# An attention and gated-MLP kernel with its whole instruction order given as a table instead of being planned at build time

## The chip, the cores and the metric

The kernel runs on one core of one Trainium2 chip. The metric is the device time of one execution in microseconds (us); lower is better. Three runs of the kernel before gave 678.15, 683.24 and 683.33 us, median 683.24 us.

## What is computed

One transformer layer on 2048 tokens of width 512, attention (32 heads of 16) and a gated MLP (hidden width 1792) side by side on the same normalised input, both added to the input:

```python
qkv = (x @ wqkv).reshape(B, S, 3, H, Dh).transpose(2, 0, 3, 1, 4)
scores = jnp.einsum("bhqd,bhkd->bhqk", q, k) * (Dh ** -0.5)
o = jnp.einsum("bhqk,bhkd->bhqd", softmax(scores), v)
attn = o.transpose(0, 2, 1, 3).reshape(B, S, D) @ wo
...
gate = x @ W_gate;  gate = gate * (gate > 0)
mlp = (gate * (x @ W_up)) @ W_down
...
xn = layernorm(x);  return x + attn(xn) + mlp(xn)
```

## The kernel before

**Tiling.** Queries are cut into 4 stretches of 512 columns (`c4`), heads into 4 groups of 8 (`gg`), each group into even and odd heads (`ee`), keys into 16 tiles of 128 (`kt`). That makes 32 blocks `(c4, gg, ee)` of 16 key tiles. For one key tile of one block, four heads are done side by side: four scores of 128 keys x 512 queries.

**Two ways to the exponential.** Most key tiles go through ScalarE (ACT): a *unit* is two of the four scores, put in one of two pairs of PSUM banks (`P_sc`, unit `u` uses pair `u % 2`), and one `activation(Exp)` of 128 x 1024 turns it into bfloat16 in a ring (L1546). There are 704 units. The other key tiles, 160 of 512, go through VectorE (DVE) and GpSimd (POOL): four evictions shift and clip a score into 16-bit integers whose bits are those of a bfloat16 (L1502, 640 of them), and two further additions (L1516 on POOL, a few on DVE at L1519) make shifted copies; all three patterns are multiplied with v, so that their sum approximates the exponential.

**TensorE (PE).** Every matmul of the stretch in the middle is on a quarter-wide tile, 64 rows x 32 columns, and loads its weights by separate instructions: four matmuls and four weight loads make one operation of the graph (L141 is the helper that records each of these matmuls; weight loads are at L1482 for scores, L1454 for the products with v, L934 for projections, MLP and output). An operation uses the upper or the lower 64 rows, and two operations on different halves can run together. A weight load is left out where the half still holds the same weights.

**Background work.** Between the units run projections of q and k, the MLP (`glu`), and output rows (`out_rows`), handed out in slots along the units. After each pair of blocks there is a chain of small steps, `normalise`: evict the sums to `o_sb` (L1364), DMA the row sums out (`rsum`, L1382 and L1388), merge even and odd heads by DMA (L1396), take reciprocals (L1403), DMA these into `rb` (L1405), spread them over partitions on DVE (L1417) and multiply (L1420). A q projection ends with an eviction and eight DMAs of 16 rows into `qT` (L982). All of these DMAs are issued from one queue, SyncE's (SP).

**What sets the order.** The kernel first records a graph: operations with an engine, a duration in ns, tiles read and written, a priority. `Graph.run` (L216) then plays a list scheduler over it at build time. It walks a model clock, takes on each engine the ready operation with the best key, picks buffer slots for tiles as it goes, and appends to one queue per engine. Its model has, for instance, 216 ns for an operation of PE, 917 ns for an exponential and a wire model for DMAs. `Graph.emit` works out which semaphore waits are needed for that order and writes the five instruction streams. Each engine executes its stream in order. `run` may also put single blank matmuls ("fill", L1564) into early gaps of PE; there are 7 in the program.

The score operation of unit `u` must wait until ACT has read unit `u - 2`, since both use one pair of banks. So on PE, every unit's scores carry a semaphore wait on ACT, and the work behind them in PE's stream waits too.

Of the kernel before, what the change touches and what calls it, by code (L numbers as in the profile page):

```python
# [49 lines left out]
EARLY = ()  # L50
# [4 lines left out]
TOGETHER = 0  # L55
# [32 lines left out]
QUADS = [0, 2, 5, 5, 6, 6, 4, 5, 6, 5, 5, 5, 6, 5, 5, 8, 5, 5, 4, 6, 6, 4, 6, 5, 5, 5, 5, 5, 5, 6, 5, 5]  # L88

# [43 lines left out]
class Op:  # L133
    __slots__ = ("eng", "dur", "fn", "deps", "order", "prio", "acq", "name", "idx", "start", "end",
                 "done", "left", "users", "signal", "sem", "val", "waits", "stream", "lat", "seq", "cseq", "hb", "after", "mode", "half", "bank", "urgent", "slack", "port",
                 "load", "wsrc", "wkey", "wwaits", "pair", "held")
# [9 lines left out]
class Graph:  # L146
# [5 lines left out]
    SWITCH = 107.0  # L152
    TO_POOL = 110.0
    ISSUE = 16.0
    FILL = 425.0
    NEAR = 20
    OWN = 90.0
    DMA_SLACK = 1000
    FILL_MIN = 230.0
    AHEAD_LOADS = 4  # L160
    EARLY = True
    REUSE = 5
    WIRE_LAT, WIRE_KB = 1300.0, 6.1
    WARM_AT, COLD = 7300.0, 2.0

    def __init__(self):
        self.ops = []
        self.fillers, self.nfill, self.twins = [], 0, []
        self.units = {}
# [46 lines left out]
    def run(self):  # L216
        ops = self.ops
        for o in ops:
            o.users = []
            o.held = []  # L220
        for t in {t for o in ops for t in o.acq} | {c for o in ops for t in o.acq for c in t.pool.cur if c is not None}:
            us = set(t.w + t.r)
            t.left = len(us)
            for o in us:
                o.held.append(t)
        for o in ops:
            if o.after is not None and int(o.after) > 0:
                o.order.add(self.units[min(int(o.after), len(self.units)) - 1])
            pre = set(o.deps) | o.order
            o.left = len(pre)  # L230
            for d in pre:
                d.users.append(o)
        cand = {e: [] for e in self.ENGS}
        free = {e: 0.0 for e in self.ENGS}
        self.queue = {e: [] for e in self.ENGS}
        for o in ops:
            if o.left == 0:
                cand[o.eng].append(o)
        n = 0

        def slot_for(t):

            best, second = None, None
            for i in (t.allowed if t.allowed is not None else range(len(t.pool.cur))):
                c = t.pool.cur[i]
                if c is None:
                    at = 0.0
                else:
                    at = release.get(c)
                    if at is None:  # L250
                        if c.left:
                            continue
                        at = release[c] = max(u.end for u in c.w + c.r)
                if best is None or at < best[0]:
                    best, second = (at, i), best
                elif second is None or at < second[0]:
                    second = (at, i)
            if t.pool.shared:
                held = any(c is not None and c.open > 0 for c in t.pool.cur)
                if t.extra:  # L260
                    if t.extra.slot is None:
                        return None
                elif t.open:
                    if held and not (self.EARLY and second is not None):
                        return None
                elif len(t.allowed) > 3 and (not held or any(b.slot is None and b.extra.slot is not None for b in self.twins)):
                    return second
            return best


        pe = {"mode": "full", "at": -1e9, "free": [0.0, 0.0]}
        last = {}

        known, release = {}, {}

# [8 lines left out]
        def ready(o):  # L284
            at = known.get(o)
            if at is None:
                at = known[o] = bound(o)
# [1314 lines left out]
```

## Time and profile before

| | |
|---|---|
| median of 3 runs | 683.24 us (678.15 to 683.33) |
| time of the profiled execution | 683.3 us |
| its span, first to last instruction | 681.3 us |
| granted TensorE clock | 1.000 |
| PE busy | 669.6 us (98%), 22355 matmuls |
| PE weight loads | 410.7 us (60%), 20975 |
| ACT busy | 659.9 us (97%), 721 instructions |
| DVE busy | 591.3 us (87%), 1001 |
| POOL busy | 334.6 us (49%), 345 |
| DMA, mean of the span | 42 GB/s |

Busy time is the union of the intervals in which an engine has an instruction under way, as the profiler records them. For matmuls the ends are modelled, so a busy PE is not a PE that streams at its peak. "Idle before" is the time between the end of an engine's last instruction and the start of the next, put down to what released it; "issue" means that the engine waited for nothing that the profile shows. A line of the timeline merges neighbours of one kind: start, length, engine, line, operation, tiles, and after the `x` how many.

### The profile page before, as it was taken

Reading aid. Unit: us, or ns where it says so; the run is one execution under the profiler, and the core shown is the slowest. Engines: PE = TensorE matmul, PEld = TensorE weight load, DVE = VectorE, ACT = ScalarE, POOL = GpSimd, SP = SyncE. Lnnn points to the kernel's source line nnn. Section 1 sums busy time; section 2 is a strip of 40 time slices with the busy share of each in tenths; the row PEclk is TensorE's granted clock in tenths of the full one; section 3 lists DMA queues with packets and bytes.
Section 4 is the critical chain, followed back from the end, with each engine's and each line's share of the span. In section 5 each row is a group of like instructions: output and inputs, shape, how many; then the busy total and the mean of one; then the engine's idle time right before and its main releaser. Section 6 shows DMA issues by size and latency. Waiting matters only on the chain.

```text
span 681.3 us, 46196 instructions
## 1 busy us (share of the span) xinstructions
PE 669.6 (98%) x22355; PEld 410.7 (60%) x20975; DVE 591.3 (87%) x1001; ACT 659.9 (97%) x721; POOL 334.6 (49%) x345
## 2 busy tenths in 40 slices
PE   8999999999999999989999999999999999999997
PEld 3456576565575765656665665556565666666664
DVE  8948999998998887989999788899989877889886
ACT  7999999999999999999999999999999999999995
POOL 3301445554455554645555564655456644435640
PEclk9999999999999999999999999999999999999999
DMA  7511011132201021110101011011200122120001
GB/s 217 79 37 28 19 39 39 40 95 67 86 12 28 24 63 36 26 47 12 45 4 36 27 49 49 24 25 28 52 6 17 32 59 60 42 52 21 23 13 34
DMA packets 51479, 28.78 MB, mean 42 GB/s; under 512 B 18840, under 2 KB 50328, under 8 KB 51288
## 3 DMA queue, kind: packets, MB, share of 16 engines
q1 hardware_dynamic: 51144, 25.70, 14.7%
q8 instruction: 169, 2.77, 1.8%
q14 instruction: 22, 0.18, 0.1%
q10 hardware_dynamic: 144, 0.13, 0.1%
HBM read 18.22 MB, written 2.10 MB: 30 GB/s over the span
## 4 chain that ended last, share of the span: by engine, by line
PE 94%; DVE 4%; DMA 1%; issue 1%; POOL 0%; DVEq 0%; SPq 0%
PE ps L141 94%; DVE qd L1502 1%; DVE stats L831 1%; DMA rb<-rrec 1%; DMA x_sb<-in_A_x_dram 0%; DVE xn_sb L854 0%; DVE mv L833 0%; DVE up_sb L1151 0%; DVE xnT L899 0%; PE ps L1275 0%; DVE qT L1086 0%; DVE xn_sb L1319 0%; DVE hT L1155 0%; DVE kT L992 0%; DVEq L605 0%
## 5 line engine op out<-in xcount | busy, mean ns | idle before, releaser
L1546 ACT ACTIVATE ring<-ps 128x1024 bf16<-128x1024 f32 x704 | 651.9, 1063 | 9.6 <-PE ps L141 8.4
L141 PE MATMUL ps<-qT,kT 64*32 64x512 bf16 x8192 | 473.6, 375 | 3.6 <-DVE qd L1502 1.8
L1516 POOL INT64_ADD qd<-qd x312 | 321.8, 1042 | 305.7 <-DVE qd L1502 189.2
L1502 DVE TENSOR_SCALAR qd<-ps 128x512 int16<-128x512 f32 x640 | 418.8, 684 | 52.1 <-PE ps L141 46.9
L141 PE MATMUL ps<-qd,v_aug 64*32 64x512 bf16 x3840 | 306.7, 375 | 0.5 <-issue 0.2
L141 PE MATMUL ps<-ring,v_aug 64*32 64x512 bf16 x2816 | 245.3, 375 | 0.8 <-issue 0.7
L1482 PEld LDWEIGHTS <-kT 64*32 64x32 bf16 x8164 | 182.2, 92 | 105.7 <-issue 26.1
L1454 PEld LDWEIGHTS <-v_aug 64*32 64x32 bf16 x5304 | 132.6, 92 | 58.9 <-issue 7.4
L141 PE MATMUL ps<-xnT,wus 64*32 64x512 bf16 x1792 | 136.4, 375 | 0.0
L141 PE MATMUL ps<-xnT,wgs 64*32 64x512 bf16 x1792 | 136.0, 375 | 0.1
L141 PE MATMUL ps<-Wd,hT 64*32 64x512 bf16 x768 | 59.5, 375 | 0.2 <-issue 0.2
L934 PEld LDWEIGHTS <-hT 64*32 64x32 bf16 x1792 | 45.8, 92 | 22.2 <-issue 3.9
L934 PEld LDWEIGHTS <-wgs 64*32 64x32 bf16 x1792 | 44.4, 92 | 22.3 <-issue 4.4
L934 PEld LDWEIGHTS <-wus 64*32 64x32 bf16 x1792 | 45.1, 92 | 19.5 <-issue 3.0
L141 PE MATMUL ps<-Wk,hT 64*32 64x512 bf16 x512 | 43.0, 375 | 0.0
L1151 DVE COPY up_sb<-ps 128x512 f32<-128x512 f32 x56 | 38.3, 684 | 5.3 <-PE ps L141 5.1
L1155 DVE SCALAR_TENSOR_TENSOR hT<-ps,up_sb 128x512 bf16<-128x512 f32 x56 | 38.2, 682 | 3.6 <-PE ps L141 3.4
L141 PE MATMUL ps<-Wv,hT 64*32 64x512 bf16 x512 | 40.3, 376 | 0.2 <-issue 0.2
L141 PE MATMUL ps<-xnT,Wq 64*32 64x512 bf16 x480 | 39.3, 375 | 0.0
L141 PE MATMUL ps<-Wo_p,x_sb 64*32 64x512 bf16 x480 | 37.8, 376 | 0.0
L141 PE MATMUL ps<-xnT,Wk 64*32 64x512 bf16 x480 | 35.7, 375 | 0.3 <-DVE xnT L899 0.3
L141 PE MATMUL ps<-Wv,xnT 64*32 64x512 bf16 x512 | 33.0, 375 | 0.4 <-issue 0.2
(83 smaller groups left out, 221.9 us busy)
## 6 DMA issues: line engine op xcount, KB each, us to landing
wus<-in_B_W_up_dram SPq DMA_DIRECT2D x38, 128.0 KB, 2.6
wgs<-in_B_W_gate_dram SPq DMA_DIRECT2D x38, 128.0 KB, 3.0
xr_sb<-in_A_x_dram SPq DMA_DIRECT2D x16, 128.0 KB, 2.3
qT<-qf SPq DMA_DIRECT2D x120, 16.0 KB, 2.5
o_sb<-o_sb SPq DMA_DIRECT2D x60, 32.0 KB, 2.5
out_dram<-xn_sb SPq DMA_DIRECT2D x15, 128.0 KB, 1.8
x_sb<-in_A_x_dram SPq DMA_DIRECT2D x8, 128.0 KB, 2.8
Wd<-in_B_W_down_dram SPq DMA_DIRECT2D x6, 128.0 KB, 2.3
```

What stands on the lines that cost most here:

```text
L141: return e.add_instruction(mybir.InstMatmult(name=e.bass.get_next_instruction_name(), engine=mybir.EngineType.PE, ins=[e.lower_ap(x), e.lo ...
L831: G.op("DVE", 580, lambda e, m=m: e.bn_stats(stats[:, m, :], xs(m)), reads=[t_xm[m]], writes=[t_st], prio=pr, order=last_xn if m == 4 and ...
L934: e.ldweights(w()[rows, 32 * j:32 * j + 32], tile_position=(rows.start, 32 * j))
L1151: G.op("DVE", 603, lambda e: e.tensor_copy(up_sb[:, tup.slot, :], bank_of(tu)), reads=[tu], writes=[tup], prio=-590)
L1155: G.op("DVE", 603, lambda e: e.scalar_tensor_tensor(out=hT[:, th.slot, :], in0=bank_of(tg), scalar=0.0, in1=up_sb[:, tup.slot, :], op0=ALU ...
L1454: e.ldweights(vs(j), tile_position=(64 * half, 32 * j))
L1482: e.ldweights(ks(m), tile_position=(64 * half, 32 * m))
L1502: G.op("DVE", 601, lambda e, j=j, tx=tx: e.tensor_scalar(qd[:, tq.slot, 512 * j:512 * j + 512], ps[:, BANK[tx.slot], :], IBIAS[3], 0.0, op ...
L1516: G.op("POOL", POOL_NS, lambda e, x=x, n=n: e.int64_add(x().bitcast(I64), raw().bitcast(I64), SHIFTS[n + 1] * LANES), reads=[ti, tq, t_lib ...
L1546: exp_ops[u] = G.op("ACT", ACT_NS, lambda e, tr=tr, k0=k0: e.activation(ring[:, tr.slot, :, :], ps[:, 4 * k0:4 * k0 + 2, :], ACTF.Exp, sca ...
```

## The change

The graph is recorded as before, operation for operation. `Graph.run`, its model constants and its tie-breaking rules are gone. In their place stands `Graph.follow`, which takes two tables: `ORDER`, the numbers of all operations in the order in which they are to be appended to the queues (`-1` is a blank matmul), and `SLOTS`, one character for each tile that needs a buffer, the number of the slot. It appends, and adds the dependences that follow from reusing slots and banks. `emit` is the same but for an unused line. The tables were worked out off line, with the fetch of TensorE's program in blocks counted in; how is not in the kernel.

```diff
-TOGETHER = 0
...
+ORDER = [
+    0, 3, 19, 1, 9, 51, 2, 4, 5, 10, 20, 7, 6, 14, 8, 17, 21, 22, 23, 24, 52, 25, 11, 53, 56, 26, 27, 54, 57, 60, 55, 28, 64, 58, 61, 68, 29, 59, 62, 65,
...
+SLOTS = [int(c, 36) for c in (
...
-    def run(self):
...
+    def follow(self, order, slots):
         self.queue = {e: [] for e in self.ENGS}
+        last, port, slots = {}, None, iter(slots)
+        for i in order:
+            if i < 0:
+                o = Op()
+                o.eng, o.fn, o.name, o.half, o.bank, o.urgent, o.stream, o.port = "PE", self.filler, "fill", None, None, 0, None, False
+                o.deps, o.order, o.acq = {}, set(), []
+                o.load, o.wsrc, o.wkey, o.wwaits, o.pair = None, (), None, (), None
+                self.ops.append(o)
+            else:
+                o = self.ops[i]
+            e = o.eng
             for t in o.acq:
                 if t.slot is not None:
                     continue
+                t.slot = next(slots)
+                c = t.pool.cur[t.slot]
                 if c is not None:
                     for u in c.w + c.r:
+                        if u.eng != e or e not in ("PE", "ACT"):
                             o.deps[u] = True
+                t.pool.cur[t.slot] = t
+            if e == "PE" and o.half is not None:
+                was = last.get(o.bank)
+                if was is not None and was.half != o.half:
+                    o.deps[was] = True
+                last[o.bank] = o
+            if o.port:
+                if e == "POOL" and port is not None:
+                    o.deps[port] = True
+                if e == "DVE":
+                    port = o
             o.seq = len(self.queue[e])
             self.queue[e].append(o)
...
-        G.fillers = [(P_b, 0, "pvz", blank_early, "full")]
-        G.run()
+        G.filler = blank_early
+        G.follow(ORDER, SLOTS)
         G.emit(nc, es)
```

Compared stream by stream, the two programs have the same instructions: 22354 recorded matmuls on both sides, 20860 separate weight loads before and 20888 after (reuse falls differently), 7 blank matmuls on both, 104 separate semaphore instructions on PE before and 128 after, the same 718 activations in the same order on ACT, the same operations on DVE, POOL and SP. The order differs on PE, DVE, SP and, slightly, POOL, from the first microseconds on. On SP, the eight `qT` DMAs of a projection, which mostly stood together before, are now mixed with weight loads and with the DMAs of `normalise`.

273 lines of the change are left out of this document (28 added, 245 removed), and 314 rows, old and new, of the table ORDER.

## The prediction

> **What bounds the kernel now.** I read the page's first part, then ACT's timeline over the whole span, then the waits.
>
> ```profile
> PE 669.6 (98%) x22355; PEld 410.7 (60%) x20975; DVE 591.3 (87%) x1001; ACT 659.9 (97%) x721; POOL 334.6 (49%) x345
> ```
>
> ```profile
> 620.00:640.00 20.00, 20.00 (x724) 12.78 (x672) 17.81 (x29) 20.00 (x23) 11.37 (x11) 1.00 0.05 13
> ```
>
> PE looks full (98%), but that is a busy time with modelled ends. In the windows of 20 us, the densest full one got 724 matmuls through (the first x). At that pace all 22355 would take 22355 / 724 x 20 = 618 us. The exponentials take longer, as these lines of ACT's timeline show (start, length, line, count, idle before):
>
> ```profile
> 10.32 1.96 ACT L1546 ACTIVATE ring<-ps 128x1024 bf16<-128x1024 f32 x2
> 12.44 1.02 ACT L1546 ACTIVATE ring<-ps 128x1024 bf16<-128x1024 f32 x1 [0.17 <-PE ps L141]
> 13.92 4.73 ACT L1546 ACTIVATE ring<-ps 128x1024 bf16<-128x1024 f32 x5 [0.46 <-PE ps L141]
> 19.21 12.95 ACT L1546 ACTIVATE ring<-ps 128x1024 bf16<-128x1024 f32 x14 [0.55 <-PE ps L141]
> 32.32 3.77 ACT L1546 ACTIVATE ring<-ps 128x1024 bf16<-128x1024 f32 x4 [0.17 <-PE ps L141]
> ...
> 131.57 36.33 ACT L1546 ACTIVATE ring<-ps 128x1024 bf16<-128x1024 f32 x39 [0.22 <-PE ps L141]
> 169.17 56.54 ACT L1546 ACTIVATE ring<-ps 128x1024 bf16<-128x1024 f32 x61 [1.27 <-PE ps L141]
> ...
> 264.17 11.46 ACT L1546 ACTIVATE ring<-ps 128x1024 bf16<-128x1024 f32 x12 [0.54 <-PE ps L141]
> ...
> 294.11 122.16 ACT L1546 ACTIVATE ring<-ps 128x1024 bf16<-128x1024 f32 x132 [1.61 <-PE ps L141]
> ...
> 604.16 67.61 ACT L1546 ACTIVATE ring<-ps 128x1024 bf16<-128x1024 f32 x73 [0.15 <-PE ps L141]
> 672.24 0.66 ACT L1291 ACTIVATE up_sb<-ps 128x256 f32<-128x256 f32 x2 [0.47 <-PE ps L141]
> ```
>
> ```profile
> 348.64 11.11 ACT L1546 ACTIVATE ring<-ps 128x1024 bf16<-128x1024 f32 x12
> ```
>
> ```profile
> 358.59 3.00 ACT L1546 ACTIVATE ring<-ps 128x1024 bf16<-128x1024 f32 x3
> ```
>
> ```profile
> ACT ring L1546 <- PE ps L141: 8.4, 20, 1.6
> PEld L1482 <- issue: 26.1, 84, 2.1
> PEld L934 <- issue: 18.8, 60, 1.0
> PEld L1454 <- issue: 7.4, 31, 0.5
> ```
>
> The span falls into a head of 10.3 us (before the first exponential), a stretch of 704 exponentials from 10.32 to 604.16 + 67.61 = 671.77, that is 661.45 us, and a tail of 681.3 - 671.8 = 9.5 us. The last two small timelines give ACT's own pace. The twelfth exponential of the run that begins at 348.64 begins at 358.59, so 11 steps take 9.95 us, 0.905 each; one alone takes 1.02 (row at 12.44), since neighbours overlap. Were ACT always fed, the stretch would take 1.02 + 703 x 0.905 = 637.2 us. So 24.2 us of it are lateness, and PE, which feeds ACT, is what ACT waits for. The kernel is bound by ACT (637 of 661), and the 24 us are PE arriving late although its sum (618) would fit. That is a question of order, which is what the change touches.
>
> Lateness has two parts. Twenty stops are visible: 8.4 us idle, and each also loses the overlap, 1.02 - 0.905 = 0.115 us, so 8.4 + 20 x 0.115 = 10.7 us. The other 13.5 us lie inside the runs: the run of 132 takes (122.16 - 1.02) / 131 = 0.925 a step, not 0.905.
>
> **What lies behind the stops.** Weight loads (PEld) are idle with nothing to wait for ("issue") 84 + 60 + 31 = 175 times, 52.3 us. Two of these, and then the stream between them and the program's own DMA queue:
>
> ```profile
> 168.76 0.09 PEld L934 LDWEIGHTS <-wgs 64*32 64x32 bf16 x4 [0.67 <-issue]
> ```
>
> ```profile
> 263.33 0.37 PE L141 MATMUL ps<-ring,v_aug 64*32 64x512 bf16 x1 [0.47 <-issue]
> 263.33 0.09 PEld L934 LDWEIGHTS <-hT 64*32 64x32 bf16 x4 [0.97 <-issue]
> ```
>
> ```profile
> 263.33:416.25 152.92, 150.37 (x5134) 94.12 (x4824) 136.31 (x223) 150.17 (x163) 84.51 (x82) 1.00 0.13 32
> ```
>
> ```profile
> q8 instruction: 169, 2.77, 1.8%
> ```
>
> ```profile
> 416.25 0.40 PE L141 MATMUL ps<-qT,kT 64*32 64x512 bf16 x4 [0.46 <-issue]
> ```
>
> At 263.33 PE stands still inside a group of four matmuls, before the fourth, where the program has no wait. From there to a stop of the same kind at 416.25 it issues 5134 + 4824 = 9958 instructions, 38.9 times 256. Queue 8 moves (packets, MB, share) 169 pieces, 2.77 MB / 169 = 16.4 KB; 22355 + 20975 instructions over 169 are 256 each. So PE's program comes in blocks of 256, and at some block edges PE waits for the next. One edge comes each 152.92 / 39 = 3.92 us, that is per 4.3 exponentials. The stop of ACT at 169.17 follows the stall at 168.76, that at 264.17 the one at 263.33. Going through the timeline, 15 of the 20 stops, from 32.32 to 604.16, stand within 1.5 us behind such a stall.
>
> Of the other five, three are in the head's wake (12.44, 13.92, 19.21), one (131.57) is small, and one, 1.61 us at 294.11, is something else:
>
> ```profile
> 283.37 6.13 SPq L982 DMA_DIRECT2D qT<-qf  x6
> 289.54 1.24 SPq L1405 DMA_DIRECT2D rb<-rrec  x2
> ```
>
> ```profile
> 292.09 0.01 DVE L1417 LOAD_MASK_SELECT rb<-rb  x1 [2.01 <-DMA rb<-rrec]
> ```
>
> ```profile
> PE ps L141 <- DVE qd L1502: 1.8, 1, 1.8
> ```
>
> SP's queue issued six `qT` DMAs in 6.13 us, the `rb` DMA stood behind them, DVE waited 2.01 us for it with evictions queued behind, PE waited 1.8 us for an eviction, ACT 1.61 for PE.
>
> **The change, part by part.** *Work.* Nothing is removed. 28 more weight loads of 0.09 us (row at 168.76) overlap matmuls; 24 more semaphore instructions and these make 52 / 256 = 0.2 block. Cost nothing, hidden by PE's 661 - 618 = 43 us of room; uncovered, 28 x 0.09 = 2.5 us.
>
> *Head and tail.* The first score stands at the same place in PE's stream and ACT's order is equal; after the last score PE has 16 instructions more. I leave 10.3 and 9.5 as they are, bounds plus or minus 0.3 (16 of 256 of 3.92 us).
>
> *Block edges.* The 15 stops: 10.7 less the five others. Those are 0.17 + 0.46 + 0.55 and 1.61 from the rows, and 0.22 at 131.57, so 3.01 + 5 x 0.115 = 3.6 us. That leaves 7.1. An order cannot remove a fetch; it can only let the score that ACT needs be past the edge. In the program before, 62 of 169 edges fall within 16 instructions behind a score's wait on ACT; in the changed one 35 of 170. So the order does know where the edges lie. I keep 35 / 62 of 7.1, that is 4.0: saved 3.1. Bounds: nothing (the stalls merely fall elsewhere) and 7.1.
>
> The Trainium skill, page "Runtime: NRT & Kernel Launch", section "Instruction fetch mechanics", says that engines stream 16 KiB blocks of 256 instructions and that crossing a block edge is mostly hidden. The size agrees with queue 8's row; the "hidden" does not agree with the 0.97 us at 263.33. By that rule this term would be 0 and the sum 677.1; by the rows it is 3.1 and the sum 674.0.
>
> *Inside the runs.* 13.5 us, PE late by less than a full stop. Here the load between scores counts. Of the intervals between scores' waits on PE, 59 of 699 had 80 instructions or more, against an average near 61; now 36 of 702. Stretches of four intervals with 268 or more: 74, now 54. The share kept is between 36 / 59 = 0.61 and 54 / 74 = 0.73; I take 0.67, saved 4.5. Bounds: nothing (evenness was not the cause) and 13.5 x 0.39 = 5.3.
>
> ```profile
> L1502 DVE TENSOR_SCALAR qd<-ps 128x512 int16<-128x512 f32 x640 | 418.8, 684 | 52.1 <-PE ps L141 46.9
> ```
>
> *SP's queue and the normalise chain.* Moved past each other: the `qT`, weight, `o_sb` and `rb` DMAs. With `qT` no longer in eights the six in a row before `rb` go; and DVE now has 7 to 14 operations between reciprocal (L1403) and spread (L1417), 5 to 10 before, mostly evictions of 418.8 / 640 = 0.65 us. I take the stop at 294.11 as gone: saved 1.61 + 0.115 = 1.7. Bounds: plus 1.7, and minus 1.7 for a second such stop elsewhere.
>
> *Sum.* 3.1 + 4.5 + 1.7 = 9.3 saved. Span 681.3 - 9.3 = 672.0; the execution adds 683.3 - 681.3 = 2.0, so **674.0 us**. The profiled execution (683.3) is at the median of the runs (683.24), so nothing is to be corrected. Best of all bounds, 7.1 + 5.3 + 1.7 = 14.1: 669.2. Worst, 0 + 0 - 1.7: 685.0. If ACT never waited: 683.3 - 24.2 = 659.1, the floor.
>
> **Rivals.** *The order nearly empties the lateness.* If scores stand ahead of every edge and every long interval, only the head's three stops (1.18 + 0.35 = 1.5 us) and a quarter of the 13.5 in the runs (3.4) stay: 659.1 + 4.9 = 664. For it: PE's 43 us of room. Against it: an interval of 80 instructions is still 80 / 256 x 3.92 = 1.2 us for 0.905 of ACT, and 36 of them stay.
>
> *The change doesn't do what it says.* The stalls are hidden where they are hidden and fall on other scores otherwise; only 1.7 us of the DMA stop go: 683.3 - 1.7 = 681.6. For it: 169 edges and only 15 stops, so most are harmless already and shifting them is a lottery. Against it: 62 to 35.
>
> *Slower: PE's stream stops at late producers.* The table fixes an order against planned times. Where DVE, 87% busy, or a DMA is later than planned, PE waits in order and ACT behind it, as at 294.11. Each costs 1.7 us. With the rest as forecast, six undo the gain (674.0 + 10.2 = 684), and ten, one for every third of the 32 blocks, reach 691. For it: nearly all of DVE's and SP's order is new. Against it: before, there was one such stop, and the distance from reciprocal to spread grew.
>
> **How the numbers follow.** A measurement of this kernel can hardly tell less than 1% (6.8 us; the three runs lie 5.2 apart) from no change: below 676.4 is faster, above 690.1 slower. Forecast (668 to 680) 0.45, of which 0.40 below 676.4; emptied 0.20, all faster; stays 0.20, all within 1%; slower rival 0.15, of which 0.12 above 690.1. So faster 0.60, within 1% 0.05 + 0.20 + 0.03 = 0.28, slower 0.12. Range 664 to 685: it takes in the worst of the bounds and leaves out half of the emptied case's lower side (0.07) and most of the slower one (0.13).
>
> **What would show it.** Right: ACT's stops fall from 20 with 8.4 us to about 12 with 4 to 5; the "issue" idle of weight loads stays near 52 us (edges are as many) while fewer ACT stops stand behind it; long runs go from 0.925 to about 0.918 a step; the wait of DVE for `rb` nearly vanishes; head and tail stay. Wrong: if the "issue" idle itself shrinks a lot, the order changes the fetch and not only what stands behind it; if ACT waits through PE for DVE or DMA in many places, the slower rival is true; if stops and runs are as before, order was not the cause of the 24 us.

## The result and the profile after

The changed kernel takes 699.86 us (median of 6 runs, 698.06 to 700.94), the kernel before, on the same chip, 682.18 us (6 runs, 678.15 to 683.33). The ratio is 1.0264, 95% interval 1.0234 to 1.0295: slower by 17.7 us, where 674.0 us was forecast. The profiled execution took 699.12 us, 15.8 more than that of before (683.3); the rows below are set against that one.

The first rows are from its page: the span, the busy times, the group of exponentials (busy and mean ns, then idle before them), and the queue that fetches programs.

```profile
span 697.1 us, 46234 instructions
...
PE 684.9 (98%) x22355; PEld 389.1 (56%) x21003; DVE 598.9 (86%) x1001; ACT 668.1 (96%) x721; POOL 334.0 (48%) x345
...
q8 instruction: 170, 2.79, 1.7%
...
L1654 ACT ACTIVATE ring<-ps 128x1024 bf16<-128x1024 f32 x704 | 660.2, 1038 | 16.7 <-PE ps L481 13.8
```

ACT's timeline of the changed kernel (start, length, count, idle before), the first exponentials, two long runs, the last ones and what follows:

```profile
10.49 2.94 ACT L1654 ACTIVATE ring<-ps 128x1024 bf16<-128x1024 f32 x3
...
59.02 58.08 ACT L1654 ACTIVATE ring<-ps 128x1024 bf16<-128x1024 f32 x62 [0.24 <-PE ps L481]
...
548.42 46.96 ACT L1654 ACTIVATE ring<-ps 128x1024 bf16<-128x1024 f32 x50 [0.44 <-PE ps L481]
...
682.61 4.83 ACT L1654 ACTIVATE ring<-ps 128x1024 bf16<-128x1024 f32 x5 [0.20 <-PE ps L481]
688.00 0.66 ACT L1405 ACTIVATE up_sb<-ps 128x256 f32<-128x256 f32 x2 [0.56 <-PE ps L481]
```

The head is 10.5 us (10.3 before) and the tail 697.1 - 682.61 - 4.83 = 9.7 us (9.5). All of the loss lies in the stretch of exponentials: 687.44 - 10.49 = 676.95 us, 15.5 more than the 661.45 before. Its lateness over 637.2 us is 39.7 us where it was 24.2. The longest stops are gone, but the runs are slower: the one of 62 takes (58.08 - 1.02) / 61 = 0.935 us a step and the one of 50 takes 0.938, against 0.925 in the run of 132 before.

The waits of the changed kernel (total us, times, longest):

```profile
DVE qd L1615 <- PE ps L481: 54.0, 134, 1.4
PEld L1595 <- issue: 29.5, 110, 0.7
PEld L1048 <- issue: 28.7, 112, 0.7
ACT ring L1654 <- PE ps L481: 13.8, 46, 0.8
PEld L1567 <- issue: 13.1, 54, 0.6
...
DVE rb L1531 <- DMA rb<-rrec: 0.5, 1, 0.5
```

Two rows of the kernel before, to set beside them:

```profile
DVE qd L1502 <- PE ps L141: 46.9, 97, 1.1
DVE rb L1417 <- DMA rb<-rrec: 3.1, 3, 2.0
```

ACT now stops 46 times, not 20, but never longer than 0.8 us (1.6 before). DVE too waits for PE oftener, 134 times for 97. "Issue" idle of weight loads grew to 29.5 + 28.7 + 13.1 = 71.3 us in 276 places, while the blocks fetched went only from 169 to 170. So many small things went wrong, all of them on the way out of PE, and as far as these rows show DMA has no part in it.

**What the trace adds when it is laid beside the program.** The table gives the order of PE's operations and the trace their starts, so each start can be put to its operation. Three things in the order differ. In the changed kernel 197 of 704 units have their two scores *split* by 1 to 4 other operations (none before). Operations follow one on the *same half* 2056 times in 5560 (640 before). *Tight handoffs*, where a bank goes from one half to the other within three operations, are 74 (40 before). PE also gets less done. The next rows show its stream from 60 to 660 us, first before, then in the changed kernel (the first x counts matmuls):

```profile
60.00:660.00 600.00, 595.51 (x20288) 370.81 (x18968) 532.66 (x867) 592.82 (x642) 320.79 (x311) 1.00 0.14 37
```

```profile
60.00:660.00 600.00, 595.35 (x19804) 342.50 (x18564) 525.01 (x845) 586.91 (x628) 312.96 (x308) 1.00 0.14 37
```

Operations of four matmuls follow each other on a busy half every 0.213 us. With four matmuls an operation and two halves, a half stands idle for 600 - 19804 / 8 x 0.213 = 72.7 us in the mean, 59.8 before.

### The profile page after: what moved, and what is told of

Read it like the earlier page. It is cut to its first block, busy times and chain, and to the rows that moved or that the text cites. A ratio compares the mean times of both kernels' runs of the same rounds, so it can differ in the third digit from the quotient of the medians.

```text
span 697.1 us, 46234 instructions
## 1 busy us (share of the span) xinstructions
PE 684.9 (98%) x22355; PEld 389.1 (56%) x21003; DVE 598.9 (86%) x1001; ACT 668.1 (96%) x721; POOL 334.0 (48%) x345
## 4 chain that ended last, share of the span: by engine, by line
PE 93%; DVE 3%; ACT 2%; DMA 1%; issue 1%; SPq 0%; POOL 0%
PE ps L481 92%; ACT ring L1654 2%; DVE qd L1615 1%; DVE stats L945 1%; DMA xnT<-xn_sb 1%; SPq L975 0%; DMA x_sb<-in_A_x_dram 0%; DVE xn_sb L968 0%; DVE hT L1269 0%; DVE xnT L1013 0%; PE ps L1389 0%; DVE mv L947 0%; PE ps L1672 0%; DVE up_sb L1265 0%; DVE xn_sb L1307 0%
## 5 line engine op out<-in xcount | busy, mean ns | idle before, releaser
L1654 ACT ACTIVATE ring<-ps 128x1024 bf16<-128x1024 f32 x704 | 660.2, 1038 | 16.7 <-PE ps L481 13.8
L481 PE MATMUL ps<-qT,kT 64*32 64x512 bf16 x8192 | 478.7, 374 | 4.9 <-ACT ring L1654 1.7
L481 PE MATMUL ps<-qd,v_aug 64*32 64x512 bf16 x3840 | 300.2, 375 | 0.1
L481 PE MATMUL ps<-ring,v_aug 64*32 64x512 bf16 x2816 | 241.7, 375 | 0.5 <-issue 0.4
L1595 PEld LDWEIGHTS <-kT 64*32 64x32 bf16 x8152 | 174.4, 92 | 115.5 <-issue 29.5
L1567 PEld LDWEIGHTS <-v_aug 64*32 64x32 bf16 x5344 | 129.5, 92 | 67.3 <-issue 13.1
L1048 PEld LDWEIGHTS <-hT 64*32 64x32 bf16 x1792 | 43.2, 92 | 25.1 <-issue 4.2
L481 PE MATMUL ps<-Wv,hT 64*32 64x512 bf16 x512 | 43.4, 375 | 0.0
L481 PE MATMUL ps<-xnT,Wq 64*32 64x512 bf16 x480 | 37.2, 374 | 0.1
```

The lines of the kernel that those rows point to most:

```text
L481: return e.add_instruction(mybir.InstMatmult(name=e.bass.get_next_instruction_name(), engine=mybir.EngineType.PE, ins=[e.lower_ap(x), e.lo ...
L1048: e.ldweights(w()[rows, 32 * j:32 * j + 32], tile_position=(rows.start, 32 * j))
L1567: e.ldweights(vs(j), tile_position=(64 * half, 32 * j))
L1595: e.ldweights(ks(m), tile_position=(64 * half, 32 * m))
L1654: exp_ops[u] = G.op("ACT", ACT_NS, lambda e, tr=tr, k0=k0: e.activation(ring[:, tr.slot, :, :], ps[:, 4 * k0:4 * k0 + 2, :], ACTF.Exp, sca ...
```

## The experiments

The experiments ran in five groups, each on a chip of its own and together with the kernel before, which took 681.4, 683.2, 676.6, 676.1 and 681.9 us there; so ratios are compared. My first theories: A, split pairs bring the loss, since ACT gets both scores later; B, rows of the same half bring it, since one half starves. The rival to both was the prediction's slower one, late producers.

### A score pair kept together: e1_join

```diff
+    def joined(self, order):
+        out = []
+        for i in order:
+            o = self.ops[i]
+            if i < 0 or o.pair is None:
+                out.append(i)
+            elif self.ops[i + 1].pair == o.pair:
+                out += [i, i + 1]
+        return out
...
+        order = self.joined(order)
```

> The changed kernel's table, with one edit when it is followed: the second score of a unit is placed right behind the first on PE (in the table 197 of 704 units have 1 to 4 other operations between the two; before, none had). Theory A, the split pairs: in the trace of the changed kernel the 193 split units past the head carry 25.3 us of lateness (start-to-start of exponentials over 0.905 us), the 499 whole ones 12.1 us, 0.024 each. Made whole, the 193 would carry 4.7: 20.6 us less, about 679 us, stops of ACT from 46 to about 25. Theory B, operations of one half of the rows standing in a row (2056 of 5560 in the table, 640 before; 1950 in this kernel): hardly a change, 694 to 700. Theory C, the edges of program blocks or DMAs: no change, 697 to 701.

Measured: 699.47 us, ratio 1.0266 (1.0227 to 1.0305).

```profile
ACT ring L1665 <- PE ps L481: 13.5, 39, 1.4
```

The stops stay: 13.5 us in 39 places. Theory A in its simple form falls: putting the second score right behind the first gives nothing here.

### The pairs of the kernel before split: e2_apart

```diff
+            n = int(APART[o.pair]) if second else 0
+            if n:
+                held.append([n, i])
+                continue
+            out.append(i)
+            if i >= 0 and o.eng == "PE" and held:
+                held[0][0] -= 1
+                if not held[0][0]:
+                    out.append(held.pop(0)[1])
```

> The order of before, written as a table and followed (the same instructions and waits as before), with one edit: in the same 197 units as in the changed kernel the second score is moved behind the next 1 to 4 operations of PE, the same number for each. Theory A: 193 units gain 0.131 - 0.033 = 0.098 us each (mean lateness of split units after, of all units before), 19 us, so about 701 us. Theory B: operations of one half in a row go from 640 to 952, (952 - 640) / (2056 - 640) of the 17.7 us, 4 us: 686. Theory C: 682.

Measured: 692.73 us, ratio 1.0172 (1.0147 to 1.0196); ACT's stops are these:

```profile
ACT ring L1678 <- PE ps L487: 10.7, 34, 1.0
```

That lies between theory B's 686 and theory A's 701. In a good order the same 197 splits cost 692.73 - 681.41 = 11.3 us, 0.057 each. (Two more units are split by the scores that were moved.) The second score of a split unit starts 0.20 us behind the first in the mean of this trace, that of a whole unit 0.06 us. So a split can cost, but the changed kernel loses more, and e1_join shows that its loss does not hang on splits alone.

### Rows of the same half in the kernel before: e3_doubled

```diff
+            if plain and a.half == c.half != b.half == d.half and not {order[at[k + 1]], order[at[k + 2]]} & new and b not in c.deps and b not in c.order:
+                order[at[k + 1]], order[at[k + 2]] = order[at[k + 2]], order[at[k + 1]]
```

> The order of before as a table, with one edit: where four operations of PE that are no scores alternate between the halves of the rows, the middle two are swapped, so that two of one half follow each other (operations of one half in a row: 1374 instead of 640; in the changed kernel 2056). All score pairs stay whole. Theory A: no change, 681 to 684. Theory B: (1374 - 640) / (2056 - 640) of 17.7 us, so 682 + 9 = 691.

Measured: 682.36 us, ratio 1.0011 (0.9986 to 1.0036), with rows of the same half up from 640 to 1374. Theory B falls: a half does not starve behind such rows, since operations on the other half can start ahead of what is listed before them (rows at 201.22 below). The swap spared scores and an accumulation's last operations ("fin"); that turned out to matter.

### Neighbours moved, all else kept: e4_near and e5_near

For the next kernels I replayed the five streams with the times that the traces show (0.213 us for an operation of PE on its half, 0.20 us from its end to ACT or DVE, 0.05 us back), and moved operations of PE to places near by where the replay ended earlier. Everything else, slots included, stays. Here and below a cut from the table shows the numbers of PE's operations alone, in their order; those of other engines between them are left out. Around unit 197 (2384 and 2385 are its scores):

```diff
-    2365, 2366, 1871, 1873, 2330, 2312, 2384, 2304, 2241, 2239, 2385, 2389,
+    2365, 2366, 1871, 1873, 2312, 2384, 2304, 2385, 2330, 2241, 2239, 2389,
```

> The changed kernel, with operations of TensorE alone put in other places near by: of 5586, 3534 stand elsewhere, by 1.1 places on average and 12 at most; ACT, DVE, POOL and SP keep the changed order, and no tile has another slot. In the new places 74 handoffs of a bank between halves within three operations become 58, returns of a bank through DVE within nine operations fall from 97 to 48, and split score pairs from 197 to 134. Theory N (neighbours): the 17.7 us that the change costs lie in what stands next to what on TensorE, so most of them come back: 676 to 686 us. Rival M (arrangement): they lie in when the jobs, evictions and DMAs come, which stays, so little comes back: 695 to 700 us.

and in the kernel before:

```diff
-    2366, 2328, 1873, 2330, 2304, 2312, 2384, 2385, 2239, 2241, 2389, 2390,
+    2365, 2366, 2328, 1871, 1873, 2304, 2384, 2312, 2385, 2330, 2239, 2241,
```

> The kernel before as a table, with operations of TensorE alone put in other places near by in the same way: 3210 of 5586, by 1.0 place on average and 12 at most; every other engine keeps the order of before. Returns of a bank through DVE within nine operations fall from 84 to 56; but 117 score pairs are now split and handoffs between halves within three operations rise from 40 to 57. Theory N (neighbours as a whole, with the splits only where there is room): 672 to 680 us, less than both kernels. Theory S (a split pair or a tight handoff costs by itself, wherever it stands, as in the kernel with 197 split pairs that lost 11.3 us): 117 / 197 of 11.3 is 6.7 us more, 686 to 690 us. Rival M (arrangement): 681 us, plus or minus 2.

Measured: 690.62 us for e4_near, ratio 1.0107 (1.0065 to 1.0148), and 691.30 us for e5_near, 1.0106 (1.0062 to 1.0150). The first missed both of its ranges (N up to 686, M from 695) and fell between them. Part of both is a longer tail, which I had not counted when I chose the places; ACT's timeline of e4_near ends like this:

```profile
652.77 24.38 ACT L1652 ACTIVATE ring<-ps 128x1024 bf16<-128x1024 f32 x26 [0.39 <-PE ps L479]
680.26 0.66 ACT L1403 ACTIVATE up_sb<-ps 128x256 f32<-128x256 f32 x2 [3.12 <-PE ps L479]
```

The last exponential ends at 677.15 of a span of 691.1: a tail of 13.9 us, 4.4 more than before (e5_near ends in the same way). Its stretch is 10.6 us shorter than the changed kernel's, by moves of 1.1 places in the mean, so most of the loss does lie with neighbours on PE. But e5_near, which the same replay had improved, got slower, by somewhat more than theory S gave its split pairs. The replay lacked something that costs both.

### What the replay lacked: reports in the order of the list

I compared each start in the traces with what the replay would make of it. PE's own starts agreed with it. What did not agree was when ACT and DVE began behind PE. So I took every ACT and DVE instruction from 40 to 665 us that had been ready but for PE, the operations of PE that it depends on, and their ends (start of the last of the four matmuls plus 0.213 us). In the kernel before 418 of 421 begin 0.20 us behind the end of their own operation, with 7 ns more in the median. In the changed kernel 207 of 562 begin later than that, 0.24 us in the median. Each of these had its operation listed behind another one, on the other half, that ended later, and began when that one had ended too. Here is one, in PE's timeline and then ACT's, of the changed kernel:

```profile
201.22 0.48 PE L481 MATMUL ps<-qT,kT 64*32 64x512 bf16 x8
201.44 0.38 PE L481 MATMUL ps<-ring,v_aug 64*32 64x512 bf16 x4
201.66 0.60 PE L481 MATMUL ps<-qd,v_aug 64*32 64x512 bf16 x8
```

```profile
199.17 2.85 ACT L1654 ACTIVATE ring<-ps 128x1024 bf16<-128x1024 f32 x3
202.34 1.94 ACT L1654 ACTIVATE ring<-ps 128x1024 bf16<-128x1024 f32 x2 [0.32 <-PE ps L481]
```

The eight matmuls at 201.22 are both scores of unit 197; the second, on the upper half, started at 201.33 and had ended by 201.55. ACT was free from 202.02. But the second score is listed (above: 2385) behind three products with v on the lower half (2304, 2241, 2239), which the row at 201.44 and the two operations in the row at 201.66 are; the last started at 201.87 and ended at 202.09. The exponential began at 202.34, 0.25 us behind *that* end and 0.79 behind its own score's.

The trace also keeps when each semaphore, the counter that a waiter watches, is raised. The one that this exponential waits for is raised for the second score at 202.32, 0.77 us after that score's end and 0.23 us after the end of the last product. In the changed kernel 104 units have their second score listed behind an operation that ends later, and in all 104 the semaphore is raised at least 0.198 us after that later end; in the kernel before there is no such unit, and 0.18 to 0.23 us after the score's own end is usual.

So PE does not start its list in order, but it reports in order, which corrects what the description of the kernel says ("Each engine executes its stream in order"). Since the ends of matmuls are modelled, the traces can't tell whether such a score is done early and reported late, or finishes late; for those who wait it is the same. This is theory R.

### The edges of the blocks moved: e6_edges

This ran with e4_near and e5_near, for the prediction's term on block edges.

```diff
-            for _ in range(10):
-                ins = e.matmul(ps[:, BANK[0], :], Wo_l[:, 0, 0:128], zeros, start=True, stop=True)
+            for _ in range(74):
+                ins = e.matmul(ps[:, BANK[0], 0:69], Wo_l[:, 0, 0:128], zeros[:, 0:69], start=True, stop=True)
```

> The changed kernel, with the warm-up matmuls on zeros at the start cut into 74 of 69 columns where there were 10 of 512: 128 more instructions on TensorE, as many columns, so that every later edge of a program block falls half a block from where it was. Nothing else is changed. Theory F (the order is fitted to the edges): the fit is spoilt. What the change saved at the edges comes back, 3 us by the idle time of the halves near edges (4.0 to 1.0 us), or as much as the 7.1 us of the prediction: 702 to 707 us. Rival (where the edges fall is nearly indifferent): 698 to 701 us.

Measured: 701.88 us, ratio 1.0273 (1.0235 to 1.0310), beside 1.0264 (1.0234 to 1.0295) without the shift. Every edge now falls half a block from where it fell when the order was worked out, and nothing changes that this measurement can tell. A loss of 7.1 us would have shown; one of 3 us is at the rim of the two intervals. The traces say more. I counted PE's instructions and took the time between the starts of two neighbours at every edge (every 256th, counted so that the stall at 263.33 is one). In the trace of before 43 of 169 edges have a gap of over 0.15 us, 0.097 us in the mean of all edges; in the changed kernel it is 24 of 170 and 0.048 us, here 23 and 0.056 us. So PE stands less at the edges than before, but nearly as little where the edges fall elsewhere as where the order was made for them. Theory F finds no support: the order's fit to the edges is worth little.

### Listed as they start: e7_started, and places chosen anew: e8_pairs

```diff
-    2365, 2366, 1871, 1873, 2330, 2312, 2384, 2304, 2241, 2239, 2385, 2389,
+    2365, 2366, 1871, 2330, 1873, 2312, 2384, 2385, 2304, 2241, 2239, 2389,
```

> The changed kernel, with TensorE's operations listed in the order in which they started in its own trace: 1892 of 5586 stand elsewhere, by one place nearly all and by three at most, and every other engine keeps the changed order. Nothing is asked to start at another time than it did; tight handoffs between halves stay as they were (74 before, 75 now), split pairs fall from 197 to 116, and rows of the same half from 2056 to 930. Theory R (reports come in the order of the program): in the changed kernel's trace, 207 of the 562 ACT and DVE instructions that had waited for TensorE began only after an operation listed earlier on the other half had ended too, 0.24 us (median) later than their own operation's end explains; in the kernel before 3 of 421 did. If TensorE reports an operation done only when those listed ahead of it are done, listing them as they start takes these away, and most of the 17.7 us come back: 681 to 690 us. Rival H (tight handoffs and late producers): these are as before, so at most the 81 pairs that come together count, 81 x 0.057 = 4.6 us: 695 to 699 us. Rival M (arrangement of the jobs and the other engines' order): 698 to 701 us.

For e8_pairs the places in the kernel before were chosen as for e5_near, with reports in the order of the list put into the replay:

```diff
-    2366, 2328, 1873, 2330, 2304, 2312, 2384, 2385, 2239, 2241, 2389, 2390,
+    2365, 2366, 2328, 1871, 2304, 1873, 2384, 2385, 2312, 2239, 2241, 2330,
```

> The kernel before as a table with TensorE's operations put in other places near by (3104 of 5586, 0.9 places on average, 12 at most), as in the earlier kernel of this kind, but with no score pair split, with reports in program order counted in when the places were chosen, and with the work behind the last exponential counted too. Returns of a bank through DVE within nine operations fall from 84 to 48, rows of the same half rise from 640 to 1702. Theory R: places chosen so that no waited-for operation is listed behind one that ends later bring the gain that the earlier kernel of this kind missed: 673 to 680 us, less than both kernels. Rival H or M: the same as the earlier one without its 117 split pairs (6.7 us) and its longer tail (5 us): 679 to 684 us. If rows of the same half cost by themselves: above 686 us.

Measured: e7_started 679.74 us beside 676.64, ratio 1.0046 (1.0023 to 1.0069). Of the 2.64% that the change costs, 2.18% are gone, 14.8 us, by listing operations of PE in the order in which they had run anyway, by three places at most. At the pace of the chip that ran the change this is 1.0046 x 682.2 = 685.3 us, inside theory R's range; rivals H (tight handoffs, which were left) and M wanted at least 695 us. The same moves also made 81 split pairs whole, which at e2_apart's price would be 4.6 us of it at most. Unit 197 in this kernel, PE and then ACT:

```profile
195.34 0.43 PE L479 MATMUL ps<-qT,kT 64*32 64x512 bf16 x8
195.61 0.38 PE L479 MATMUL ps<-ring,v_aug 64*32 64x512 bf16 x4
195.82 0.60 PE L479 MATMUL ps<-qd,v_aug 64*32 64x512 bf16 x8
```

```profile
195.15 5.63 ACT L1652 ACTIVATE ring<-ps 128x1024 bf16<-128x1024 f32 x6
```

The three products run behind the scores as before, the last until 195.82 + 0.22 + 0.21 = 196.25. The exponential of unit 197 is the second of ACT's run, so it begins at 195.15 + 0.905 = 196.05, without a gap and before they end: its scores are now listed ahead of them. And the waits of the whole kernel:

```profile
DVE qd L1613 <- PE ps L479: 45.5, 110, 1.1
...
PEld L1593 <- issue: 24.0, 88, 1.0
PEld L1046 <- issue: 19.1, 74, 0.9
...
PEld L1565 <- issue: 9.0, 46, 0.3
ACT ring L1652 <- PE ps L479: 6.8, 14, 1.0
```

ACT's stops fall from 13.8 us in 46 places to 6.8 in 14, below the 8.4 in 20 of before (whose trace is of another chip, on which that kernel takes longer). The "issue" idle of weight loads falls with them, from 71.3 to 52.1 us, with the same 170 blocks. From 60 to 660 us PE gets 20388 matmuls through, which leaves a half idle for 600 - 20388 / 8 x 0.213 = 57.2 us.

e8_pairs: 675.86 us, ratio 0.9990 (0.9970 to 1.0009). It does not lose e5_near's 1.06%, but the gain that theory R promised for it (680 us or less; it is 0.9990 x 682.2 = 681.5 at the pace of the other chip) did not come; 681.5 lies in the range of rivals H and M.

### Waited-for operations listed late: e9_listed

If theory R is true, the kernel before must get slower by nothing more than a listing one place later. One of the 219 places, and the same kind of swap that cost nothing in e3_doubled:

```diff
-    3137, 2923, 2952, 2925, 2954, 3120,
+    3137, 2923, 2925, 2952, 2954, 3120,
```

> The kernel before as a table, with 219 operations of TensorE listed one place later, and nothing else: each is one that ACT, DVE, POOL or an operation on the other half waits for, and it changes places with the next one, which is on the other half and in the trace of before ran later. Its half is free, so it can start as before; only its place in the list falls behind an operation that ends up to 0.21 us later. Theory R (reports come in the order of the program): up to 219 reports come late, 0.1 us each in the mean, about half of the 44 us of late reports of the changed kernel, whose removal brought 14.6 us: 3 to 7 us slower than before, a ratio of 1.004 to 1.010. Rival (it starts at the same time, so the list does not matter, as when 734 pairs of operations that mostly nobody waited for were swapped): a ratio of 0.998 to 1.002.

Measured: 678.37 us beside 676.14, ratio 1.0039 (1.0020 to 1.0059), 2.6 us slower and just below the range that theory R gave; the rival's range (up to 1.002) touches only the end of the interval. Fewer reports came late than I thought, 23, with 2.9 us (0.5 us before), since most of these waiters had time.

### How far neighbours alone reach: e10_before_replaced and e11_after_replaced

Both choose PE's places anew, pairs together, with handoff times drawn out a little. Around unit 197, first for the kernel before, then for the changed one:

```diff
-    2366, 2328, 1873, 2330, 2304, 2312, 2384, 2385, 2239, 2241, 2389, 2390,
+    2328, 2365, 2366, 2304, 1873, 2312, 2384, 2385, 2239, 2330, 2241, 2389,
...
-    2365, 2366, 1871, 1873, 2330, 2312, 2384, 2304, 2241, 2239, 2385, 2389,
+    2328, 2365, 2366, 1871, 1873, 2312, 2384, 2385, 2304, 2241, 2330, 2239,
```

> The kernel before as a table, TensorE's operations in other places near by (2979 of 5586, 0.9 places on average, 15 at most), no score pair split, places chosen with reports in program order and with handoff times drawn out by up to 0.05 us, so that they hold when the chip is a little late. Theory R: less than before by 0 to 6 us, a ratio of 0.991 to 1.000. Rival (the earlier kernel of this kind, ratio 0.999, is what the order of neighbours can give): 0.997 to 1.002.

> The changed kernel, TensorE's operations in other places near by (3569 of 5586, 1.1 places on average, 17 at most), all score pairs but one together, places chosen with reports in program order; every other engine keeps the changed order. Theory R: all of the 17.7 us lay in neighbours on TensorE, so the ratio to before falls from 1.026 to 0.99 to 1.00, below the 1.005 of the kernel that only lists operations as they start. Rival M (3 us of the loss lie in the arrangement of the jobs and the other engines' order): 1.002 to 1.007.

Measured: e10 676.86 us, ratio 1.0014 (0.9995 to 1.0033), in its rival's range; e11 676.22 us, ratio 1.0000 (0.9982 to 1.0019), at the upper end of theory R's and clear of M's. The waits of e11:

```profile
DVE qd L1613 <- PE ps L479: 42.3, 94, 1.5
...
ACT ring L1652 <- PE ps L479: 4.4, 11, 1.0
```

e11 has the changed kernel's order on ACT, DVE, POOL and SP and the changed arrangement of the jobs, and loses nothing. e10, chosen in the same way from the order of before, comes to 1.0014, so the choosing brought the order of before nothing; if it brought the changed order no more, it hides no loss. So the 17.7 us lie, within the intervals, in the order of neighbours on PE, and rival M falls. But no order of neighbours that I found beats the kernel before, though e10's range reached down to 0.991; why is open. That ACT stops less in e11 (4.4 us in 11 places) than in the trace of before is no gain of its order: on this chip e9_listed, nearly the order of before and 2.6 us slower than it, stops even less.

```profile
ACT ring L1652 <- PE ps L479: 2.1, 4, 0.7
```

### The fetch counted in by the planner of before: e12_counted

```diff
+            if e == "PE" and o.half is not None:
+                n0 = pe["n"]
+                pe["n"] = n0 + 4 + (0 if held0[o.half] == o.wkey else 4)
+                if (pe["n"] - 193) // 256 > (n0 - 193) // 256:
+                    fetch = 100.0
...
+                if fetch:
+                    pe["free"] = [max(f, at + o.dur) + fetch for f in pe["free"]]
```

> The kernel before, with its own planner, which now counts 0.1 us in which both halves stand still after every 256th instruction of TensorE, as much as an edge cost in the mean in the trace of before (0.097 us over 169 edges). The order comes out anew on every engine; no score pair is split; rows of the same half rise from 640 to 1040, tight handoffs between halves from 40 to 69. Theory F (counting the fetch brings the gain of the prediction's block edges, 3.1 us): a ratio to before of 0.993 to 0.997. Theory R: what counts is how many waited-for operations are listed behind one that ends later, and this planner does not see that either; with 400 more rows of the same half than before where the changed kernel has 1416 more, it loses about a quarter of the 17.7 us: a ratio of 1.003 to 1.010. No difference, 0.998 to 1.002: neither matters at this size.

Measured: 700.27 us, ratio 1.0270 (1.0234 to 1.0306). Every range missed it. It says nothing about theory F's 3 us, since another loss of 18 us covers them, and R does not explain that loss: only 7 of 384 waiting instructions had a late report. ACT stops seldom, but long:

```profile
ACT ring L1559 <- PE ps L141: 23.4, 23, 2.3
```

```profile
123.38 29.60 ACT L1559 ACTIVATE ring<-ps 128x1024 bf16<-128x1024 f32 x32 [1.81 <-PE ps L141]
154.48 11.11 ACT L1559 ACTIVATE ring<-ps 128x1024 bf16<-128x1024 f32 x12 [1.50 <-PE ps L141]
167.09 138.28 ACT L1559 ACTIVATE ring<-ps 128x1024 bf16<-128x1024 f32 x150 [1.50 <-PE ps L141]
```

The runs between are good (the one of 150: (138.28 - 1.02) / 149 = 0.921 a step), and every so often the planner comes out with nothing for ACT for 1.5 to 2.3 us. That is another loss of the same size, by chance. Perhaps the planner's many constants hold for the old plan alone; that was not tried.

### All runs side by side

"Late reports" are the waiting ACT and DVE instructions, as counted above, that an operation listed earlier held up by over 0.02 us, and by how much in all.

| kernel | ratio to before | late reports | split pairs | same half | tight handoffs |
|---|---|---|---|---|---|
| before | 1 | 3, 0.5 us | 0 | 640 | 40 |
| the change | 1.0264 | 207, 44.4 | 197 | 2056 | 74 |
| e1_join | 1.0266 | 137, 27.2 | 0 | 1950 | 80 |
| e2_apart | 1.0172 | 43, 6.7 | 199 | 952 | 48 |
| e3_doubled | 1.0011 | 26, 3.4 | 0 | 1374 | 37 |
| e4_near | 1.0107 | 150, 23.7 | 134 | 1762 | 58 |
| e5_near | 1.0106 | 136, 25.2 | 117 | 1738 | 57 |
| e6_edges | 1.0273 | 205, 45.8 | 197 | 2056 | 74 |
| e7_started | 1.0046 | 48, 6.0 | 116 | 930 | 75 |
| e8_pairs | 0.9990 | 57, 6.8 | 0 | 1702 | 45 |
| e9_listed | 1.0039 | 23, 2.9 | 0 | 992 | 50 |
| e10_before_replaced | 1.0014 | 50, 7.9 | 0 | 1578 | 43 |
| e11_after_replaced | 1.0000 | 71, 9.5 | 1 | 1562 | 52 |
| e12_counted | 1.0270 | 7, 0.7 | 0 | 1040 | 69 |

Six kernels lose under 0.5% and have 71 late reports at most; of the seven that lose 1% or more, five have 136 or more. The other columns do not sort them so: e1_join loses 2.7% with no pair split, and e8_pairs loses nothing with 1702 rows of one half. Two losses are of another kind: e2_apart's second scores do start late, and e12_counted's loss is not explained.

The column is no price list, though. e1_join has 17 us fewer late reports than the change and is no faster. What it lacks is those of the exponentials: its trace has no unit with the second score listed behind an operation that ends later, where the change has 104. DVE's waits for PE stay:

```profile
DVE qd L1626 <- PE ps L481: 56.3, 138, 1.6
```

So the exponentials' late reports, of which unit 197 is one, are not the price by themselves; which of the others cost how much was not separated.

## Why the prediction was wrong

**What bounds the kernel.** ACT waits for PE and the loss is a matter of order: that was right, and e7_started and e11 show it. Wrong was to call 661 - 618 = 43 us "room" on PE that hides what an order costs. A half does stand idle for 59.8 us of 600 before, and the changed order still lost 17.7 us.

**The reading of "issue".** I took 175 such idle times for 169 edges. That they were nearly as many was chance: with 170 blocks there are 276 in the changed kernel, 71.3 us, and in e7_started 88 + 74 + 46 = 208, 52.1 us. Most of them are not fetches, since only 43 of the 169 edges show a gap of over 0.15 us. But the stalls that mattered were read rightly: all 15 stops of ACT that I put down to edges stand behind an edge with a gap of 0.35 to 0.85 us.

**Work, head and tail.** Right as far as the runs tell: head and tail moved by 0.2 us each.

**Block edges (3.1 us).** The size came about, but not for the reason given, so that is luck. In the trace of before 15 stops of ACT, 5.4 us, stand within 1.5 us behind an edge with a gap of over 0.25 us (at the edge or within two instructions of it); in the changed kernel 5 do, 1.8 us. With the overlap of ten stops that is 5.4 - 1.8 + 10 x 0.115 = 4.8 us less. But in e6_edges, with every edge elsewhere, it is 6 stops and 2.3 us. So it is not the order's fit (35 edges behind a score's wait where there were 62) that spares ACT. And these stalls differ from trace to trace: in that of e9_listed, nearly the order of before on another chip, a single stop of 0.4 us stands behind an edge. The Trainium skill, page "Runtime: NRT & Kernel Launch", section "Instruction fetch mechanics", says that crossing a block edge is mostly hidden. The trace of before agrees in the mean, 0.097 us an edge, and not at the 15 edges behind which ACT stopped.

**Inside the runs (4.5 us).** This is the step that failed, together with the silent assumption that no new stops come. I counted instructions between the scores' waits, and that count did get better (59 intervals of 80 or more, then 36); yet the lateness inside the runs went from 13.5 to 39.7 - (13.8 + 46 x 0.115) = 20.6 us, and stops from 10.7 to 19.1. The stops that stand behind no edge went from 5 with 3.0 us to 41 with 12.0 us. The count took an operation as done for its waiter when PE has run it. The runs showed that it is done when all that is listed before it on either half has ended. The table's order lists operations of one half in rows (2056 times for 640) with a waited-for one behind them, and has 44.4 us of late reports for it. Listing the same operations as they start took most of them away and with them 14.8 of the 17.7 us. That PE reports in the order of the list is shown by the semaphores, and that the listing carries most of the loss by e7_started (of whose gain up to 4.6 us may belong to the 81 pairs made whole). Which of the late reports cost, and why e1_join with fewer of them gains nothing, stays open.

**SP's queue and the normalise chain (1.7 us).** Right: DVE's wait for `rb` fell to 0.5 us, once, and no other such stop took its place.

**The rivals.** The slower one gave 691 us and has the sign, but not the mechanism: it has PE stopping at late producers, DVE above all. The rows show the other direction, DVE waiting for PE 134 times, and e11 keeps DVE's and SP's order and loses nothing. The rival that the change does nothing (681.6) was right that the fit to the edges is worth little, and missed the loss. The chance of 0.12 for slower was too small since all three rivals took the order of starts for the order of reports. What I had in hand and did not count were the split pairs and the rows of one half; both stand in the table, and the first alone would have said that ACT gets a second score up to four operations later 197 times.

## What to carry to other kernels

Where an engine runs parts of itself side by side, read from the trace not only when an operation starts but also when its waiters begin; if the two drift apart, look for an operation listed earlier that ends later. When an order is written as a table, put each waited-for operation ahead of all that ends after it: 1892 moves of one to three places, which asked no operation to start at another time, were worth 14.8 us here. And a count in the profile that nearly equals another (175 idle times, 169 edges) is no proof that they are the same things; move one of them and see whether the other follows.

## What the runs showed of the hardware

- TensorE's halves start ahead of each other: the second score of unit 197 started at 201.33, ahead of three operations listed before it, the last of which started at 201.87. They are reported in the order of the list: over the fourteen traces there are 963 instructions that waited for such an operation, and in 961 of them the start, less the usual 0.20 us, is not before the end of the last operation listed earlier; it is 0.05 us behind that in the median of the changed kernel. The Trainium skill, page "TensorE: Matmul & The Clock Gate", section "The mechanism", says that matmuls keep the order of the program in their starts and in their ends. For the ends, as waiters see them, the traces agree (961 of 963); for the starts, on tiles of different halves, they do not (201.33 and 201.87).
- Swapping neighbours on the two halves costs nothing that the runs can tell where hardly anybody waits (e3_doubled, ratio 1.0011, 0.9986 to 1.0036) and costs 2.6 us in 219 places where somebody may (e9_listed).
- An edge of a program block costs PE little in the mean: in the trace of before, 43 of 169 edges show a gap of over 0.15 us, and the mean is 0.097 us. But 15 of ACT's 20 stops there stand behind such an edge.
- The chips differ: the kernel before took 676 to 677 us on two of them and 681 to 683 us on the others, so times and traces from two chips are not to be set against each other without it.
